# Thirteen tiles and TensorE for half of gV in the backward pass of a decode block

## The chip, the core and the metric

The kernel runs on one core of one Trainium2 chip. Its engines are TensorE (PE in the profile; its weight loads are PEld), VectorE (DVE), ScalarE (ACT), GpSimd (POOL) and SyncE (SP). Each follows its own list of instructions in order, and semaphores join the lists. Sixteen DMA engines move data between HBM and the on-chip SBUF. SP issues the loads, POOL issues the two large writes of each head, and ACT issues the writes of the weight gradients. The metric is the device time of the program in microseconds (us); lower is better.

## The reference

A transformer block for decoding, forward and backward, with two batch entries, one query position, D = 640, 32 heads of 128, a cache of 4096 positions and a ReLU layer of width 1728:

```python
def _fwd_reference(A_x, A_k_cache, A_v_cache, A_wq, A_wo, B_x, B_w1, B_w2):
    x = A_x
    h = x + attention(layernorm(x), A_k_cache, A_v_cache, A_wq, A_wo)
    h2 = h + relu(layernorm(h) @ B_w1) @ B_w2
    return h2
# attention: q = x@wq; s = q.k * 128**-0.5; p = softmax(s); o = p.v; out = o@wo
# outputs: h2, and the gradients of <h2, grad_out> with respect to
#          A_x, A_k_cache, A_v_cache, A_wq, A_wo, B_w1, B_w2
```

Everything is bfloat16. There are 64 pairs of batch entry and head. For each pair K and V are 1 MB each and are read, and gK and gV are 1 MB each and are written. With p a row of softmax weights, `gV[s] = p[s] * go` (go is the gradient of the head's output) and `gK[s] = gs[s] * q`, where `gs[s] = p[s] * (go.V[s] - dot)` needs V again.

## The kernel before

All tiles of 128 x 4096 bf16 (1 MB) live in a list of numbered homes that change their use: `ld` for loads, `g` for gK and gV on their way out, `f` for the weight gradients on theirs, `q` for late weights. `NBIG = 12` homes exist from the start, two more when the first pass ends (`big1`), one more (`big2`) and six more (`big3`) later. A queue written out by hand (`queue`, `pump`) issues the loads in order, each as soon as a home is free.

**First pass** (`p1_iter`, one iteration `i` per pair, over 64 pairs): `pair_transpose` turns K in four groups on TensorE (four fp32 transposes into one PSUM bank, copied out by ScalarE as `t_sb`; tag `XT` in SBUF). `pair_matvec` multiplies the transposed group with q (eight small matmuls). Softmax weights `ep` follow, VectorE forms `pk = K * p` in two halves (L464), and TensorE contracts `pk` with V (L457) and with a selector (L486).

**Background work** is written as generators (`bg`, `bg2`, `bg3`) that give out a piece after each step of the main work, paced by `RATES`, `RATE2`, `RATE3` and by `slot`, the number of row sums (L644 on VectorE) allowed at a step. For each batch entry `middle_gen` runs the layer between the passes, ending with `go_group` (one row sum a head), after which the second pass may take that head. `fin_gen` forms the weight gradients as outer products on TensorE (L928), copies them out on ScalarE (L934) and writes them; `gx_gen` and `mlp_out` do the last two row results.

**Second pass** (`p2_iter`, one turn `j` per pair). The order of the turns is `turns`: in each batch entry the last `KEPT` heads come first, because their V is still in SBUF from the first pass (6 in entry 0, 5 in entry 1). The other 53 turns load V again under the name `Wt`. Turns 0 to 11 run beside the first pass, one turn to two iterations; from turn 14 on the second pass is alone. A turn does, in six steps:

1. the last matvec of the turn before (group T3) and its `gsp` (L832); two broadcast matmuls (L841) copied out scaled as `rb` (L846); on POOL `pp`, a copy of the weights (L848); transposes T0; the first half of gK of the turn before (L819, VectorE);
2. the second half of gK of the turn before and its write (L860, POOL);
3. transposes T1, matvec of T0; 4. T2, matvec of T1; 5. T3, matvec of T2, first half of gV (VectorE);
6. second half of gV and its write (L881, POOL).

In turns 14 to 32 (`act = 8`) eight of the 32 columns of gV are formed by ScalarE instead, each by one scaled copy of `rb` (L880), the scale coming from `pa`, which POOL writes (L852):

```python
        outer_half(gV, c["rb"][:, 0:128], c["pp"], 1, act)
        for k in range(act):
            nc.scalar.activation(out=gV[:, NSC - act + k, :], in_=c["rb"][:, 0:128], func=ACT.Copy, scale=pa[:, k:k + 1])
        nc.gpsimd.dma_start(out=natural(out_3, b, h), in_=gV[:])
```

POOL's list at a turn's end and the next one's start is therefore: write of gV, `pp`, `pa`, write of gK.

Of the kernel before, what the change touches and what calls it, by code (L numbers as in the profile page):

```python
# [15 lines left out]
def kernel(  # L16
# [34 lines left out]
    GT = 8  # L51
# [4 lines left out]
    NMT = (32, 12)  # L56
# [6 lines left out]


# [15 lines left out]
    NBIG = 12  # L80
# [71 lines left out]
    neg_ident = const.tile([128, 128], BF16)  # L152
    nc.vector.tensor_scalar(out=neg_ident[:], in0=ident_bf[:], scalar1=-SCALE, scalar2=None, op0=ALU.mult)
# [3 lines left out]
    sel = const.tile([128, 2, 2, 64], BF16)  # L157
    nc.gpsimd.memset(sel[:], 0.0)
    for par in range(2):
        nc.gpsimd.affine_select(out=sel[:, par, :, :], in_=sel[:, par, :, :], compare_op=ALU.not_equal,  # L160
                                fill=1.0, base=-par, pattern=[[0, 2], [-2, 64]], channel_multiplier=1)
# [17 lines left out]
    xr = cols.tile([4 * ND, 128], BF16)  # L179
# [15 lines left out]

    gom = cols.tile([128, H, B, 2, 2], BF16)
# [3 lines left out]
    Uc = cols.tile([128, B, H], FP32)  # L200
# [3 lines left out]
    P_bf = cols.tile([128, B * H, NSC], BF16)  # L204
# [5 lines left out]
    nc.sync.dma_start(out=xr[0:2 * ND, :], in_=A_x.rearrange("b s (c p) -> (b s c) p", p=128))  # L210
    nc.sync.dma_start(out=xr[2 * ND:4 * ND, :], in_=grad_out.rearrange("b s (c p) -> (b s c) p", p=128))
# [11 lines left out]
    def ln_fwd(xs, nb, xh, rstd):  # L223

        def st(name, dt=FP32):
            return small.tile([128, nb], dt, tag=f"ln_{name}{nb}", bufs=1, name=f"ln_{name}")
# [7 lines left out]
        cent = small.tile([128, nb, ND], FP32, tag=f"ln_cent{nb}", bufs=1, name="ln_cent")  # L234
        nc.vector.tensor_tensor(out=cent[:], in0=xs, in1=bc(mean[:], ND), op=ALU.subtract)
        sq = small.tile([128, nb, ND], FP32, tag=f"ln_sq{nb}", bufs=1, name="ln_sq")
# [5 lines left out]
        y_bf = small.tile([128, nb, ND], BF16, tag=f"ln_y{nb}", bufs=1, name="ln_y")  # L242
# [33 lines left out]
    def ln_bwd(gh, xh, rstd, add, dst, nb):  # L276

        def t3(name):
            return small.tile([128, nb, ND], FP32, tag=f"lb_{name}{nb}", bufs=1, name=f"lb_{name}")
# [3 lines left out]
        mm = small.tile([128, 2, nb], FP32, tag=f"lb_mm{nb}", bufs=1, name="lb_mm")  # L283
# [5 lines left out]
        nm = small.tile([128, 2, nb], FP32, tag=f"lb_nm{nb}", bufs=1, name="lb_nm")  # L289
# [25 lines left out]
    nc.tensor.transpose(x_ps[:], xr[:], ident_bf[0:4 * ND, 0:4 * ND])  # L315
# [9 lines left out]
    nc.gpsimd.memset(hot[:, H - 1:H], 1.0)  # L325
    es = pkp.tile([128, B, H], FP32)
# [7 lines left out]
    def pair_rows(dst, src, hs, bs):  # L334

        n, nb = hs.stop - hs.start, bs.stop - bs.start
        t = pst([128, 2, n, nb], FP32, "mid", "pr_ps")
        for par in range(2):
            nc.tensor.matmul(t[:, par, :, :], lhsT=sel[:, par, :, :].rearrange("p c k -> p (c k)"),
                             rhs=src[:, hs, bs], start=True, stop=True)  # L340
        for c in range(2):
            rows = slice(64 * c, 64 * c + 64)
            for par in range(2):
                nc.vector.tensor_copy(out=dst[rows, hs, bs, par, c], in_=t[rows, par, :, :])
# [26 lines left out]
    def all_q():  # L371

        zero = small.tile([128, H * B], BF16, tag="zero", bufs=1, name="zero")
        nc.vector.memset(zero[:], 0.0)
# [7 lines left out]
        nc.tensor.matmul(q_ps[:].rearrange("p h b -> p (h b)"), lhsT=ident_bf[:], rhs=zero[:], start=True, stop=False)  # L382
# [12 lines left out]
    KEPT = (6, 5)  # L395
# [4 lines left out]
    u4 = cols.tile([128, 128], FP32)  # L400
# [14 lines left out]
    def pair_transpose(nat, g, dve=False, busy=0):  # L415
# [8 lines left out]
        t_sb = mats.tile([128, GT // 2, 128], FP32, tag="XT", bufs=5, name="t_sb")  # L424
# [24 lines left out]
    def p1_iter(i, dve_group, busy):  # L449
# [48 lines left out]
        if p is not None:  # L498

            bp, hp = pairs[i - 1]  # L500
            bhp = bp * H + hp
# [41 lines left out]
        if p is not None:  # L543
            pk_tile(1)
            if hp % OG == OG - 1:
                nc.vector.reciprocal(out=rt[:, bp, hp + 1 - OG:hp + 1], in_=totp)
            (nc.gpsimd if i < P2_AT else nc.vector).tensor_copy(out=P_bf[:, bhp, :], in_=ep[:, :, 0])
            pk_half(1)
            give(p["K"], "g" if i == P2_AT else None)
# [58 lines left out]
    def u_out(b):  # L608

        t = pst([128, H], FP32, "mid", "uc_ps")  # L610
        nc.tensor.matmul(t[:], lhsT=u4[:], rhs=fold[:], start=True, stop=True)
        nc.vector.tensor_tensor(out=Uc[:, b, :], in0=t[:], in1=rt[:, b, :], op=ALU.mult)


    def bcast_cols(colsrc, n, kc_of, dst):

        for c0 in range(0, n, 4):
            t = pst([128, 512], FP32, "bc", "bc_ps")
            w = 0
            for c in range(c0, min(n, c0 + 4)):  # L620
# [4 lines left out]
            nc.scalar.copy(out=dst[:, c0 * 128:c0 * 128 + w], in_=t[:, 0:w])  # L625
            yield
# [6 lines left out]
    def store_row(col_bf, n, dst):  # L633
# [3 lines left out]
        r = small.tile([16, 128], BF16, tag="orow", bufs=2, name="orow")  # L637
# [3 lines left out]
    def ttr(in0, in1, acc, width, kc=128, junk=None):  # L641
        if junk is None:
            junk = cols.tile([128, D], BF16, tag="junk", name="junk")
# [14 lines left out]
    def go_group(b, h0, h1, hbc):  # L658
# [3 lines left out]
        go32 = small.tile([128, GH], FP32, tag="go32", bufs=1, name="go32")  # L662
        for k in range(n):
            yield from turn()
            ttr(wo_t[:, h0 + k, :], hbc[:], go32[:, k:k + 1], D)
            yield 0.9
        nc.vector.tensor_copy(out=goc[:, hs, b], in_=go32[:, 0:n])
        pr = small.tile([128, GH], FP32, tag="pr", bufs=1, name="pr")
# [12 lines left out]
        ud = small.tile([128, GH], FP32, tag="ud", bufs=1, name="ud")  # L681
        nc.vector.tensor_tensor(out=ud[:, 0:n], in0=Uc[:, b, hs], in1=negdot[:, hs, b], op=ALU.mult)
        mg = small.tile([128, GH], FP32, tag="mg", bufs=1, name="mg")
# [7 lines left out]
    def mlp_out():  # L691

        ml32 = small.tile([128, ND, B], FP32, tag="ml32", bufs=1, name="ml32")
        nc.vector.memset(ml32[:], 0.0)
        for k in range(NW2):
            while free["q"] < 1:
                yield
# [12 lines left out]
        ml_bf = small.tile([128, ND, B], BF16, tag="ml_bf", bufs=1, name="ml_bf")  # L710
        nc.vector.tensor_copy(out=ml_bf[:], in_=ml32[:])
        y_bf = small.tile([128, B, ND], BF16, tag="y_bf", bufs=1, name="y_bf")
# [6 lines left out]
    def middle_gen(b):  # L719
        if o_next[0] < (b + 1) * H // OG:  # L720
            o_group()
        nc.vector.tensor_reduce(out=u4[:], in_=u_bank[0][:].rearrange("p (s d) -> p d s", s=4),
                                axis=AX.X, op=ALU.add)
        yield
# [7 lines left out]
        at_bf = small.tile([128, ND], BF16, tag="at_bf", bufs=1, name="at_bf")  # L732
        nc.vector.tensor_copy(out=at_bf[:], in_=asum[:, b, :])
        nc.vector.tensor_tensor(out=h1c[:, :, b], in0=xg32[:, b, :], in1=at_bf[:], op=ALU.add)
        h32 = small.tile([128, 1, ND], FP32, tag="h32", bufs=1, name="h32")
# [15 lines left out]
        if b == B - 1:  # L751
            ar_ps = pst([128, NFF, B], FP32, "mid", "ar_ps")
            for cf in range(NFF):
                for c in range(ND):
                    nc.tensor.matmul(ar_ps[:, cf, :], lhsT=w1_t[:, c, bass.ds(cf, 128, step=NFF)],
                                     rhs=x2c[:, c, :], start=(c == 0), stop=(c == ND - 1))
                yield 0.25
            nc.vector.tensor_scalar(out=arow[:, 0:NFF, :], in0=ar_ps[:], scalar1=0.0, scalar2=None, op0=ALU.max)
            if F_rem:
                nc.vector.tensor_copy(out=arow[:, NFF, :], in_=acol[:, NFF, :])  # L760
        mask = small.tile([128, NF], FP32, tag="mask", bufs=1, name="mask")
# [3 lines left out]
        fbc = cols.tile([128, Dff], BF16, tag="fbc", name="fbc")  # L765
        gx2 = small.tile([128, 1, ND], FP32, tag="gx2", bufs=1, name="gx2")
        gx2p = small.tile([128, ND, 3], FP32, tag="gx2p", bufs=1, name="gx2p")
        FW = Dff // 3
        spread_f = bcast_cols(one(ghfc, b), NF, f_kc, fbc)
        have = 0  # L770
        for k in range(3):
            while have < min(Dff, (k + 1) * FW):
                next(spread_f)
                have += 512
                yield
            for c in range(ND):
                yield from turn()
                ttr(w1_t[:, c, k * FW:(k + 1) * FW], fbc[:, k * FW:(k + 1) * FW], gx2p[:, c, k:k + 1], FW)
# [4 lines left out]
        hbc = cols.tile([128, D], BF16, tag="rowbc", name="hbc")  # L783
        yield from bcast_cols(one(gh1c, b), ND, lambda c: 128, hbc)
# [10 lines left out]
    def ga_gen():  # L795

        gbc = cols.tile([128, Dff], BF16, tag="fbc", name="gbc")
        for b in range(B):
            yield from bcast_cols(one(gc, b), ND, lambda c: 128, gbc[:, b * D:(b + 1) * D])
        for k in range(NW2):  # L800
# [3 lines left out]
            for c in range(k * FP, min(NF, (k + 1) * FP)):  # L804
                kc = f_kc(c)
                for b in range(B):
                    yield from turn()
                    ttr(t[0:kc, c - k * FP, :], gbc[0:kc, b * D:(b + 1) * D], ga[0:kc, b, c:c + 1], D, kc)
# [15 lines left out]
    def p2_iter(j, busy, act=0):  # L824

        c = S2[j] if j < NP1 else None
        p = S2[j - 1] if j >= 1 else None
        if p is not None:
            bp, hp = turns[j - 1]
            pair_matvec(p["dp"], p.pop("T3"), 3, gom[:, hp, bp, :, :])  # L830
            gsp = small.tile([128, NSC, 2], BF16, tag="gsp", name="gsp")
            nc.vector.scalar_tensor_tensor(  # L832
                out=gsp[:], in0=p["dp"][:, :, None].to_broadcast([128, NSC, 2]), scalar=negdot[:, hp, bp:bp + 1],
                in1=P_bf[:, bp * H + hp, :, None].to_broadcast([128, NSC, 2]), op0=ALU.add, op1=ALU.mult)
        if c is not None:
# [9 lines left out]
            rb = mats.tile([128, 256], BF16, tag="rb", bufs=4, name="rb")  # L845
            nc.scalar.activation(out=rb[:], in_=bank[:, 128:384], func=ACT.Copy, scale=rt[:, b, h:h + 1])  # L846
            pp = small.tile([128, NSC, 2], BF16, tag="pp", name="pp")
            nc.gpsimd.tensor_copy(out=pp[:], in_=P_bf[:, b * H + h, :, None].to_broadcast([128, NSC, 2]))  # L848
            c.update(rb=rb, pp=pp)
            if act:  # L850
                pa = small.tile([128, act], FP32, tag="pa", bufs=2, name="pa")
# [388 lines left out]
```

## Time and profile before

| what | value |
|---|---|
| time, median of 3 runs | 902.24 us (900.63 to 907.04) |
| profiled execution, its span from first to last instruction | 902.8 us |
| PE, DVE, ACT, POOL busy | 757.2, 687.2, 485.8, 198.7 us |
| moved by DMA | 362.89 MB, mean 402 GB/s |
| K, V, V again (`Wt`) loads | 64, 64, 53 of 1 MB |
| gK and gV writes | 64 and 64 of 1 MB |
| other writes (`ot`) | 14.91 MB |

The span of the profiled execution is its whole time; no other time is given for it. It lies within 0.1% of the median. A busy TensorE in this table is not TensorE at its peak: a transpose that waits for its bank or its tile counts in part. Rows of the profile's parts are quoted below as they stand; a line such as L423 is a line of the kernel before.

### The profile page before, as it was taken

How to read it: one execution, taken by the hardware profiler on the slowest of the kernel's cores; microseconds unless marked ns; L12 is line 12 of the kernel's file. 1: busy time of each engine (PE TensorE's matmuls, PEld its weight loads, DVE VectorE, ACT ScalarE, POOL GpSimd, SP SyncE). 2: the span in 40 equal slices, each digit the busy share in tenths (PEclk: the TensorE clock that was granted, in tenths of full speed). 3: DMA queues.
4: the chain of work that ended last, by engine and by line, in shares of the span. 5: the costliest groups of instructions: out<-in, count | busy, mean ns of one | idle time of the engine just before them, and what ended most of it. 6: DMA issues, size and time to landing. Idle time of an engine off the chain costs nothing.

```text
span 902.8 us, 24701 instructions
## 1 busy us (share of the span) xinstructions
PE 757.2 (84%) x10205; PEld 634.2 (70%) x10205; DVE 687.2 (76%) x1286; ACT 485.8 (54%) x1248; POOL 198.7 (22%) x349
## 2 busy tenths in 40 slices
PE   3999899899999898898968876878999778959880
PEld 3888788888888787787757765656767566645560
DVE  2566788777988796697778697769798448999982
ACT  0444344344565554464536677776577656637660
POOL 1344444343311011010012141122112111111120
PEclk9999999999999999798985555555557555555555
DMA  8999999999879999999999999999999999999995
GB/s 365 426 419 414 417 402 417 424 424 377 330 310 381 415 405 424 425 416 425 404 399 399 389 410 417 417 389 388 404 413 409 425 424 424 419 425 422 423 422 240
DMA packets 56256, 362.89 MB, mean 402 GB/s; under 512 B 5680, under 2 KB 11696, under 8 KB 15312
## 3 DMA queue, kind: packets, MB, share of 16 engines
q1 hardware_dynamic: 34704, 212.18, 57.8%
q0 software_dynamic: 18432, 134.23, 35.9%
q10 hardware_dynamic: 3008, 14.91, 4.1%
q8 instruction: 80, 1.31, 0.5%
q14 instruction: 32, 0.26, 0.1%
HBM read 212.16 MB, written 149.13 MB: 400 GB/s over the span
## 4 chain that ended last, share of the span: by engine, by line
PE 49%; DMA 21%; DVE 13%; ACT 11%; issue 5%; SPq 1%; POOL 0%; ACTq 0%; POOLq 0%; DVEq 0%
PE t_ps L423 21%; PE m_ps L457 10%; DMA Vt<-in_A_v_cache_dram 10%; ACT t_sb L428 3%; ACT gV L880 3%; DMA out_dram<-gK 3%; PE s_ps L436 3%; DVE gV L819 3%; PE u_ps L486 3%; PE dp_ps L436 3%; PE o_ps L928 3%; DMA wqs<-in_A_wq_dram 3%; DVE pk L464 2%; DVE gK L819 2%; DMA Kt<-in_A_k_cache_dram 2%
## 5 line engine op out<-in xcount | busy, mean ns | idle before, releaser
L428 ACT COPY t_sb<-t_ps 128x512 f32<-128x512 f32 x479 | 273.4, 585 | 211.0 <-PE t_ps L423 205.2
L436 PEld LDWEIGHTS <-t_sb 128*128 128x128 bf16 x4096 | 181.6, 103 | 62.0 <-ACT t_sb L428 27.4
L423 PE MATMUL t_ps<-ident_f,Wt 128*128 128x128 f32 x848 | 207.2, 396 | 0.4 <-ACT t_sb L428 0.4
L457 PE MATMUL m_ps<-pk,Vt 128*128 128x129 bf16 x2048 | 171.8, 223 | 16.1 <-DMA Vt<-in_A_v_cache_dram 14.7
L464 DVE TENSOR_TENSOR pk<-Kt,ep 128x2048 bf16<-128x2048 bf16 x128 | 156.5, 1223 | 33.5 <-PE m_ps L457 15.3
L423 PEld LDWEIGHTS t_ps<-ident_f,Wt 128*128 128x128 f32 x848 | 144.1, 206 | 33.2 <-issue 27.1
L819 DVE TENSOR_TENSOR gK<-rb,gsp 128x2048 bf16<-128x2048 bf16 x128 | 152.2, 1223 | 13.1 <-DMA out_dram<-gV 10.9
L423 PE MATMUL t_ps<-ident_f,Kt 128*128 128x128 f32 x1024 | 156.7, 287 | 4.4 <-DMA Kt<-in_A_k_cache_dram 4.3
L457 PEld LDWEIGHTS <-Vt 128*128 128x128 bf16 x2048 | 125.3, 99 | 46.5 <-issue 29.7
L819 DVE TENSOR_TENSOR gV<-rb,pp 128x2048 bf16<-128x2048 bf16 (+1 forms) x128 | 142.9, 1140 | 10.9 <-DMA out_dram<-gK 6.0
L423 PEld LDWEIGHTS t_ps<-ident_f,Kt 128*128 128x128 f32 x1024 | 113.7, 145 | 8.5 <-PE s_ps L436 2.6
L474 POOL COPY pk<-ep 128x16 bf16<-128x16 bf16 x80 | 83.2, 1042 | 161.0 <-ACT ep L512 90.5
L436 PE MATMUL dp_ps<-gom,t_sb 128*128 128x2 bf16 x2048 | 96.6, 168 | 17.8 <-ACT t_sb L428 17.1
L881 POOL DMA_DIRECT2D out_dram<-gV x64 | 34.2, 534 | 304.7 <-DVE gV L819 175.4
L436 PE MATMUL s_ps<-qm,t_sb 128*128 128x2 bf16 x2048 | 87.7, 164 | 1.2 <-DVE t_sb L426 1.2
L860 POOL DMA_DIRECT2D out_dram<-gK x64 | 34.0, 532 | 222.0 <-DVE gK L819 167.9
L571 ACT CAST MT<-m_ps 128x128 bf16<-128x128 f32 x64 | 17.1, 267 | 104.4 <-PE m_ps L457 104.3
L934 ACT CAST ot<-o_ps 128x512 bf16<-128x512 f32 (+4 forms) x160 | 70.2, 489 | 2.9 <-DMA out_dram<-ot 1.5
L832 DVE SCALAR_TENSOR_TENSOR gsp<-dp_ps,negdot,P_bf 128x64 bf16<-128x64 f32 x64 | 18.0, 282 | 50.8 <-PE dp_ps L436 50.0
L644 DVE CUSTOM_DVE_ANT_0 junk<-wo_t,hbc 128x640 bf16<-128x640 bf16 x64 | 52.7, 823 | 0.2
L846 ACT ACTIVATE rb<-dp_ps,rt 128x256 bf16<-128x256 f32 x64 | 30.1, 470 | 41.1 <-PE dp_ps L841 40.4
L644 DVE CUSTOM_DVE_ANT_0 gxj<-wqs,gqr 128x1024 bf16<-128x1024 bf16 x40 | 48.8, 1220 | 1.5 <-DMA wqs<-in_A_wq_dram 1.3
(200 smaller groups left out, 779.0 us busy)
## 6 DMA issues: line engine op xcount, KB each, us to landing
Kt<-in_A_k_cache_dram SPq DMA_DIRECT2D x64, 1024.0 KB, 15.3
Vt<-in_A_v_cache_dram SPq DMA_DIRECT2D x64, 1024.0 KB, 15.3
out_dram<-gV POOLq DMA_DIRECT2D x64, 1024.0 KB, 13.1
out_dram<-gK POOLq DMA_DIRECT2D x64, 1024.0 KB, 13.9
Wt<-in_A_v_cache_dram SPq DMA_DIRECT2D x53, 1024.0 KB, 12.4
wq_t<-in_A_wq_dram SPq DMA_DIRECT2D x5, 1024.0 KB, 9.0
wo_t<-in_A_wo_dram SPq DMA_DIRECT2D x4, 1280.0 KB, 18.1
wqs<-in_A_wq_dram SPq DMA_DIRECT2D x5, 1024.0 KB, 17.1
```

The lines of the kernel that those rows point to most:

```text
L423: nc.tensor.transpose(t_ps[:, j, :], natf[:, 2 * cc:2 * cc + 2, :].rearrange("p c k -> p (c k)"), ident_f[:])
L428: nc.scalar.copy(out=t_sb[:], in_=t_ps[:])
L436: nc.tensor.matmul(dst[:, sc:sc + 2], lhsT=v[:, j, :, par], rhs=vecs[:, par, :], start=(par == 0), stop=(par == 1))
L457: nc.tensor.matmul(r["m"][:, 0:129], lhsT=r["V"][:, sc, :], rhs=r["pk"][sc // HALF][:, sc % HALF, 0:129], start=(sc == 0), stop=(sc == NSC ...
L464: nc.vector.tensor_tensor(out=p["pk"][k][:, :, 0:128].rearrange("p s (a two) -> p s a two", two=2), in0=p["K"][:, sl, :].rearrange("p s (a ...
L474: nc.gpsimd.tensor_copy(out=col, in_=e)
L644: nc.vector.tensor_tensor_reduce(out=junk[0:kc, 0:width], in0=in0, in1=in1, scale=1.0, scalar=0.0, op0=ALU.mult, op1=ALU.add, accum_out=acc)
L819: nc.vector.tensor_tensor(out=pairs_view(dst[:, sl, :]), in0=row.rearrange("p (a two) -> p a two", two=2)[:, None, :, :].to_broadcast([128 ...
L846: nc.scalar.activation(out=rb[:], in_=bank[:, 128:384], func=ACT.Copy, scale=rt[:, b, h:h + 1])
L860: nc.gpsimd.dma_start(out=natural(out_2, bp, hp), in_=gK[:])
L881: nc.gpsimd.dma_start(out=natural(out_3, b, h), in_=gV[:])
L934: nc.scalar.copy(out=ot[0:P, k, n0:n0 + nn], in_=o_ps[0:P, 0:nn])
```

## The change

1. **Thirteen tiles.** `NBIG` goes from 12 to 13. Room is made by sharing small tiles (`sm`, `rows`, `scr`), by `P_bf` with 52 slots instead of 64, by fewer buffers (`XT` 5 to 4, `rb` 4 to 3, `pp`, `gsp` 3 to 2), and by fewer copies of small constants.
2. **Six V kept in each batch entry.** `KEPT` goes from (6, 5) to (6, 6): one `Wt` load fewer (52).
3. **TensorE and ScalarE form half of gV** in turns 14 to 32. POOL writes 16 weights into `wide`; four matmuls turn them to rows (`pt_ps`), ScalarE copies these out as `pt` (in an `XT` buffer); at the turn's end four groups of four matmuls with one row of weights each make 16 columns of gV in two PSUM banks, and four ScalarE copies of 128x512 bring them to gV.
4. **Four middle sums a head**: `slot` allows a row sum at four steps of a turn up to turn 32 instead of three. The built program has the last `go_group` sum of entry 1 in turn 34, before in turn 40, and what follows it moves forward by some six turns.
5. **Turns beside the first pass** (0 to 11) finish their own gK (`p2_whole`, `p2_tail`) in the iteration without a turn of its own.
6. Smaller: the layer's transposed activations (`arow`) come from 13 two-row matmuls in `fin_gen` instead of 65 matmuls with w1; the outer products for w2's gradient use 128 rows instead of 96, and one PSUM bank instead of three until the middle is over; the two small loads of x and grad_out are issued by ACT instead of SP.

```diff
-    NMT = (32, 12)
+    NMT = (32, 10)
-    NBIG = 12
+    NBIG = 13
-    KEPT = (6, 5)
+    KEPT = (6, 6)
-        t_sb = mats.tile([128, GT // 2, 128], FP32, tag="XT", bufs=5, name="t_sb")
+        t_sb = mats.tile([128, GT // 2, 128], FP32, tag="XT", bufs=4, name="t_sb")
...
+    def p2_gs(j):
+        p = S2[j]
+        bp, hp = turns[j]
+        pair_matvec(p["dp"], p.pop("T3"), 3, gom[:, hp, bp, :, :])
+        gsp = small.tile([128, NSC, 2], BF16, tag="gsp", bufs=2, name="gsp")
...
-    def p2_iter(j, busy, act=0):
+    def p2_iter(j, busy, pe=0):
...
-            if act:
-                pa = small.tile([128, act], FP32, tag="pa", bufs=2, name="pa")
-                nc.gpsimd.tensor_copy(out=pa[:], in_=P_bf[:, b * H + h, NSC - act:NSC])
+            if pe:
+                nc.gpsimd.tensor_copy(out=wide[:, :, 0:pe // 4, 0],
+                                      in_=P_bf[:, P_slot[(b, h)], NSC - pe:NSC].rearrange("p (q t) -> p t q", t=4))
             c["T0"] = pair_transpose(c["W"], 0, busy=busy)
+            if pe:
+                pt_ps = pst([128, 512], FP32, "gv", "pt_ps")
+                for t in range(4):
+                    nc.tensor.matmul(pt_ps[:, t * 128:(t + 1) * 128], lhsT=wide[:, t, :, :].rearrange("p q x -> p (q x)"),
+                                     rhs=ident_bf[:], start=True, stop=True)
+                pt = mats.tile([128, GT // 2, 128], FP32, tag="XT", bufs=4, name="pt")[:].bitcast(BF16)
+                pt = pt.rearrange("p j k -> p (j k)")
+                nc.scalar.copy(out=pt[:, 0:512], in_=pt_ps[:])
...
-        outer_half(gV, c["rb"][:, 0:128], c["pp"], 1, act)
-        for k in range(act):
-            nc.scalar.activation(out=gV[:, NSC - act + k, :], in_=c["rb"][:, 0:128], func=ACT.Copy, scale=pa[:, k:k + 1])
+        if pe < HALF:
+            outer_half(gV, c["rb"][:, 0:128], c["pp"], 1, pe)
+        for q in range(pe // 4):
+            gv_ps = pst([128, 4, 128], FP32, "gv", "gv_ps")
+            for t in range(4):
+                nc.tensor.matmul(gv_ps[:, t, :], lhsT=pt[32 * q:32 * q + 1, t * 128:(t + 1) * 128],
+                                 rhs=c["rb"][32 * q:32 * q + 1, 0:128], start=True, stop=True)
+            c0 = NSC - pe + 4 * q
+            nc.scalar.copy(out=gV[:, c0:c0 + 4, :], in_=gv_ps[:])
         nc.gpsimd.dma_start(out=natural(out_3, b, h), in_=gV[:])
...
+    def p2_tail(j):
+        p = S2[j]
+        bp, hp = turns[j]
+        gsp = p2_gs(j)
+        yield
+        gK = take("g", [128, NSC, 128], "gK")
+        outer_half(gK, p["rb"][:, 128:256], gsp, 0)
+        yield
+        outer_half(gK, p["rb"][:, 128:256], gsp, 1)
+        nc.gpsimd.dma_start(out=natural(out_2, bp, hp), in_=gK[:])
...
+    PE_GV = 16
     MIXED = {1: 2, 3: 1, 4: 1, 6: 1}
-    REST = {1: 1}
+    REST = {1: 2, 4: 1, 6: 1}
...
+            banks.update(sps=[2, 3], gv=[4, 5], o=[])
...
-            g2 = p2_iter(j, 0, 8 if i is None and j <= H else 0)
+            if i is not None and n + 1 < len(plan) and plan[n + 1][1] is None:
+                g2 = p2_whole(j)
+            else:
+                g2 = p2_iter(j, 0, PE_GV if i is None and j <= H and not late[0] else 0)
...
-                slot[0] = int(k in ((1, 3, 5) if j <= H else (1, 4)))
+                slot[0] = int(k in ((1, 2, 3, 5) if j <= H else (1, 4)))
```

## The prediction

> **What bounds the kernel now.** I read the page's forty slices first, then the busy times by stage, then single turns of the second pass in the timeline, since the change names that pass.
>
> ```profile
> PE   3999899899999898898968876878999778959880
> PEclk9999999999999999798985555555557555555555
> DMA  8999999999879999999999999999999999999995
> GB/s 365 426 419 414 417 402 417 424 424 377 330 310 381 415 405 424 425 416 425 404 399 399 389 410 417 417 389 388 404 413 409 425 424 424 419 425 422 423 422 240
> ```
>
> The reader sees a kernel that moves data nearly always: the best slices reach 424 to 426 GB/s, and 362.89 MB at 424 would take 856 us. The 47 us between that and the span of 902.8 us are all that smoother work can win. They sit in a few places: the start, 200 to 290 us, 440 to 700 us, and the end. TensorE's granted clock falls to half at about 476 us, where the second pass is alone, and stays there.
>
> ```profile
> core 0: us, PE busy (x) PEld busy (x) DVE busy (x) ACT busy (x) POOL busy (x), PEclk, DMA share, GB/s
> 200.00:290.00 90.00, 86.43 (x1509) 76.29 (x1506) 75.01 (x193) 49.46 (x137) 19.92 (x35) 1.00 0.90 349
> 440.00:476.00 36.00, 25.16 (x408) 22.05 (x407) 27.76 (x52) 14.59 (x39) 5.28 (x11) 0.86 0.99 396
> 476.00:532.00 56.00, 46.36 (x533) 41.38 (x531) 43.99 (x86) 39.53 (x107) 14.39 (x29) 0.50 1.00 396
> 532.00:627.00 95.00, 71.37 (x657) 58.72 (x658) 75.53 (x140) 69.47 (x188) 21.17 (x47) 0.54 1.01 403
> 627.00:700.00 73.00, 67.48 (x611) 52.50 (x611) 60.70 (x106) 50.52 (x116) 15.35 (x30) 0.57 1.00 409
> 700.00:890.00 190.00, 147.80 (x1294) 108.44 (x1292) 151.91 (x206) 108.43 (x229) 28.93 (x62) 0.54 1.01 423
> ```
>
> From 700 us on nothing can be won but bytes (423 GB/s). From 200 to 290 us TensorE is the bound and DMA stands still a tenth of the time, about 16 us. The writes of gV start turn 14 at 480.2 us and turn 32 at 622.3 us, so the 19 turns that the change rebuilds (14 to 32) take 476 to 627 us, 151 us or 7.9 us a turn. A turn moves 3 MB (V in, gK and gV out), 3.15e6 bytes or 7.4 us at 424 GB/s: DMA is the bound there, with little to spare. One such turn without much background shows what the engines need:
>
> ```profile
> 517.49 0.63 PE L622 MATMUL bc_ps<-ident_bf,ghfc 128*128 128x128 bf16 x4
> 517.92 1.06 PE L423 MATMUL t_ps<-ident_f,Wt 128*128 128x128 f32 x4
> ...
> 520.53 0.40 PE L436 MATMUL dp_ps<-gom,t_sb 128*128 128x2 bf16 x8
> 520.79 1.09 PE L423 MATMUL t_ps<-ident_f,Wt 128*128 128x128 f32 x4
> 521.68 0.40 PE L436 MATMUL dp_ps<-gom,t_sb 128*128 128x2 bf16 x8
> 522.62 0.37 PE L436 MATMUL dp_ps<-gom,t_sb 128*128 128x2 bf16 x8 [0.54 <-ACT t_sb L428]
> ...
> 523.02 1.91 PE L423 MATMUL t_ps<-ident_f,Wt 128*128 128x128 f32 x8
> ```
>
> ```profile
> 518.82 0.53 POOL L881 DMA_DIRECT2D out_dram<-gV  x1 [4.39 <-ACT gV L880]
> 519.34 0.48 POOL L848 COPY pp<-P_bf 128x64 bf16<-128x64 bf16 x1
> 519.76 0.72 POOL L852 CAST pa<-P_bf 128x8 f32<-128x8 bf16 x1
> ```
>
> ```profile
> 521.98 0.58 ACT L428 COPY t_sb<-t_ps 128x512 f32<-128x512 f32 x1 [0.56 <-PE t_ps L423]
> 522.46 2.45 ACT L880 ACTIVATE gV<-rb,pa 128x128 bf16<-128x128 bf16 x8
> ```
>
> From start to next start, at half clock: four transposes 0.89 us (520.79 to 521.68), eight matvecs 0.26 us, a matvec with the two broadcasts 0.40 us (522.62 to 523.02), four 128x128 bf16 matmuls with four different weights 0.43 us (517.49 to 517.92). TensorE's turn is 4 x 0.89 + 3 x 0.26 + 0.40 = 4.7 us, and turns here come every 6.4 us. TensorE has 1.7 us over, and the scaled copies at the turn's end hold up no TensorE instruction of their own turn.
>
> **Half of gV on TensorE.** Removed per turn: 2.45 us of ScalarE, 0.66 us of VectorE (the half gV of 1024 columns) and `pa`. Added: 20 small matmuls on TensorE, 5 copies on ScalarE (0.58 us each, 0.49 us behind each other), `wide` on POOL. VectorE's gain is spent: a fourth row sum at 0.82 + 0.08 us a turn costs as much. What is new is a loop through three engines, and the built order shows each link. POOL issues the write of gV after ScalarE's last copy, then `pp`, then `wide` of the next turn; TensorE needs `wide` for the four matmuls `pt_ps`, which stand right after T0, and all of T1, T2, T3 is queued behind them. Added up from the start of `pt_ps`:
> - `pt_ps` 0.43, then three times transposes and matvec, 3 x (0.89 + 0.26) = 3.45;
> - the four groups of gV. Each is 0.43 on TensorE; with two banks group 3 waits for the copy of group 1. Copies cannot start before a result is there (0.63 with a hand-over of 0.2) and end at 1.2, 1.7, 2.5 and 2.9 us. TensorE is free after 2.2, ScalarE after 2.9;
> - POOL: 0.53 for the write, 0.50 for `pp` (mean of 64), 0.39 for `wide` (mean of `pa`, whose form is nearest), and 0.2 for hand-overs: 1.6.
> Sum 0.43 + 3.45 + 2.9 + 1.6 = 8.4 us. TensorE's own work in it is 0.43 + 3.45 + 2.2 + 0.40 + 0.89 = 7.4 us, so it waits 1.0 us a turn. Both are above the 7.4 us of DMA or equal to it, at half clock.
>
> Background adds to that. In turns 14 to 21 it is small (70 one-column matmuls, 19 broadcasts: about 6 us of TensorE in eight turns), half of it in the wait: 8.7 us a turn, 70 us. In turns 22 to 32 the built order has 14 outer products of 512 columns and 14 of 128 (0.68 and 0.36 us at half clock around 608 us), 33 matmuls of row spreading and broadcasts, and the head groups: about 26 us in eleven turns or 2.4 a turn, of which 1.0 fills the wait: 9.8 us a turn, 108 us. Together 178 us against 151: +27. The low end is TensorE's work alone with copies fully hidden, 0.43 + 3.45 + 1.72 + 1.29 = 6.9, plus background 0.75 and 2.4: 61 + 102 = 163 us, +12. The high end has POOL at its slow rows and no background hidden, 8.8 + 0.75 and 8.8 + 2.4: 199 us, +48. I take +27, since the loop is worked out link by link from neighbours of the same shape.
>
> Here a rule speaks against the change. The row first: the four broadcasts above load four different weights and still follow each other at 0.108 us, so the loads are covered. The Trainium skill ("TensorE: Matmul & The Clock Gate", section "The mechanism") says a weight load overlaps running matmuls only when its row group differs, and the four of one gV group share theirs. By its figure for 128 columns (section "LDWEIGHTS", estimate 107 ns) a group would take 0.86 us instead of 0.43; the sum by it is in the last rival. The trace does not agree for full rows, and I go by the row.
>
> **What comes back.** DMA is not the bound in those turns, so at turn 32 more is done than before: all four free `ld` homes hold loaded V instead of about half, the queue of writes is empty (a write lands 13 us after its issue now, some 2 MB queued), a larger piece of out_7 is out, and one V load fewer is left. That is 1 + 2 + 1.5 + 0.5 MB, 5 MB or 11 to 12 us at 424 GB/s in the stage that DMA bounds to the end. Bounds 5 and 14; I take 11, which holds the saved load (2.5 us).
>
> **The rest.** The thirteenth tile lets DMA run one tile further before it stands still in 200 to 290 us: 1 MB or 2.5 us, between 0 and 2.5; I take 2.5. Finishing gK in the same pair moves 2.4 us of VectorE from the iteration with a turn to the one without, with its write one iteration earlier; by the 36 us from 440 at 396 GB/s (2.4 us lost) it is worth between -4 and +4 (VectorE's 27.76 of 36 us could also queue worse); I take -2. The first load leaves SP 0.8 us earlier: between 0 and -0.8, taken as -0.8. The 65 matmuls with w1 (4.5 us of TensorE) go, in the same turns as the loop, where the background estimate leaves them out. Fewer `XT`, `rb`, `pp`, `gsp` buffers cost nothing, since in the built order the reader of each old tile stands before the next writer by a turn; were that cover gone, ScalarE would wait one matvec, 0.26 us, a turn. More outer-product rows (128 for 96) cost nothing on TensorE, which streams columns.
>
> **The sum**: 902.8 + 27 - 11 - 2.5 - 2 - 0.8 = 913.5 us; the median runs stand 0.6 us below the profiled one, so I forecast 913 us.
>
> **Rivals.**
> - *Faster: the denser work brings the clock back.* At full clock the trace has four transposes in 0.45 us and a matvec group in 0.21 (around 567 us); the loop is then 0.22 + 3 x 0.66 + 2.7 + 1.6 = 6.5 us, below DMA's 7.4, and half of the 8.5 us that 476 to 627 us lose against 424 GB/s comes back: 902.8 - 4 - 2.5 - 5.3 = 891 us. For it: the clock is full through 300 us of the first pass. Against: from 627 to 700 us TensorE is busy 67.48 of 73.00 us and the clock is 0.57. The Trainium skill ("TensorE: Matmul & The Clock Gate", "What's actually happening") has the clock return after about 3.4 us of sustained activity; by that rule these 73 us should have been at full clock, and the trace shows they mostly were not.
> - *No change:* the low end of the loop with most of it repaid: 902.8 + 12 - 8 - 5.3 = 901.5 us. For it: DMA bounds the last 200 us whatever comes first. Against: 4 MB of free homes is all that can be filled in advance.
> - *Much slower:* weight loads of one row lie open. The 2x128 loads at L928 have a mean of 138 ns; 16 of them add 2.2 us to 1.72, 1.7 more than the 2.2 counted, 32 us in 19 turns: 913 + 32 - 3 = 942 us. It decides from about 30 ns a load, where the groups outlast the copies.
>
> **How the numbers follow.** Forecast 0.42, no change 0.32, faster 0.20, much slower 0.06. A measurement of this kernel tells about 1% from no change, 893 to 911 us: the faster rival lies below, no change within; of the forecast's own spread I leave all above 911. That is faster 0.20, same 0.32, slower 0.48. The range is 891 to 934: down to the faster case, up to the loop's high end (902.8 + 48 - 12 - 5.3 = 933.5).
>
> **What would show it.** Right: writes of gV in turns 14 to 32 come 8.5 to 10 us apart; DMA below 400 GB/s in that stage and at 424 after it; `pt_ps` matmuls waiting for POOL `wide`; clock near 0.5. The thirteenth tile: more than 349 GB/s in 200 to 290 us. Wrong: turns of 8 us or less there, a clock near 1.0, or TensorE held by the gV tile's last write.

## The result and the profile after

The changed kernel takes 945.96 us (median; 945.03 to 948.80) against 902.32 us (900.63 to 907.04) for the kernel before in the same comparison: a ratio of 1.0468 [1.0439, 1.0496]. It is slower by 4.7%; the forecast was 913 us with a range to 934. The profiled execution has a span of 943.7 us against 902.8 us. The page's slices of the kernel after, two of its rows:

```profile
PEclk9999999999999999989955555555558655565556
GB/s 380 418 404 411 409 400 409 419 417 379 345 263 423 421 422 422 422 422 422 404 375 303 308 326 294 303 277 348 345 355 424 423 423 424 426 423 419 420 420 289
```

Until about 476 us and from about 700 us on transfers run much as before (411 GB/s against 419 from 10 to 200 us, 422 against 423 from 700 to 890 us). Between them, in slices 21 to 30, where the kernel before had 388 to 417 GB/s, they fall to 277 to 375. The same stretches of the kernel after as windows (columns: us, busy time and instructions of PE, PEld, DVE, ACT and POOL, granted clock, DMA share, GB/s):

```profile
200.00:290.00 90.00, 85.98 (x1494) 75.98 (x1493) 72.03 (x185) 46.41 (x128) 19.46 (x35) 0.98 0.89 349
476.00:532.00 56.00, 44.44 (x488) 36.80 (x487) 31.68 (x65) 33.67 (x63) 12.39 (x23) 0.50 0.84 326
532.00:627.00 95.00, 71.27 (x707) 56.08 (x708) 54.92 (x113) 59.50 (x123) 20.10 (x37) 0.55 0.80 310
627.00:700.00 73.00, 58.23 (x541) 45.91 (x540) 49.89 (x95) 44.01 (x91) 14.95 (x27) 0.50 0.85 327
700.00:890.00 190.00, 155.54 (x1418) 113.86 (x1417) 158.24 (x219) 116.52 (x254) 32.10 (x66) 0.58 1.01 422
```

VectorE and ScalarE have less to do from 476 to 627 us than before, TensorE is no busier, and DMA stands still a sixth to a fifth of the time: no engine is full, which points to a chain through several engines. The issue of gV's writes by POOL gives the length of it. Turn 14 and turn 32, first in the kernel before (L881), then in the kernel after (L925):

```profile
480.22 0.53 POOL L881 DMA_DIRECT2D out_dram<-gV  x1 [5.40 <-ACT gV L880]
622.27 0.53 POOL L881 DMA_DIRECT2D out_dram<-gV  x1 [4.33 <-ACT gV L880]
481.50 0.53 POOL L925 DMA_DIRECT2D out_dram<-gV  x1 [5.36 <-ACT gV L924]
670.62 0.53 POOL L925 DMA_DIRECT2D out_dram<-gV  x1 [5.74 <-ACT gV L924]
```

| write of gV | before | after | difference |
|---|---|---|---|
| turn 14 | 480.2 us | 481.5 us | +1.3 |
| from turn 14 to turn 32 (18 steps) | 142.1 us, 7.9 a turn | 189.1 us, 10.5 a turn | +47.1 |
| from turn 32 to the end of the span | 280.5 us | 273.1 us | -7.4 |

All of the loss arises in the 19 turns that form half of gV on TensorE. The end of one of them, the next one and the start of a third, in rows chosen from the timeline of the kernel after:

```profile
489.83 2.40 DVE L841 TENSOR_TENSOR gK<-rb,gsp 128x2048 bf16<-128x2048 bf16 x2
490.08 0.53 POOL L925 DMA_DIRECT2D out_dram<-gV  x1 [4.51 <-ACT gV L924]
490.60 0.55 POOL L878 COPY pp<-P_bf 128x64 bf16<-128x64 bf16 x1
491.08 1.25 POOL L881 COPY wide<-P_bf 128x16 bf16<-128x16 bf16 x1
492.40 0.61 PE L887 MATMUL pt_ps<-ident_bf,wide 128*128 128x128 bf16 x4 [1.84 <-POOL wide L881]
496.27 0.62 PE L921 MATMUL gv_ps<-rb,pt 1*128 1x128 bf16 x8
497.55 1.07 PE L921 MATMUL gv_ps<-rb,pt 1*128 1x128 bf16 x8 [0.66 <-ACT gV L924]
499.54 0.53 POOL L925 DMA_DIRECT2D out_dram<-gV  x1 [6.48 <-ACT gV L924]
500.06 0.25 POOL L878 COPY pp<-P_bf 128x64 bf16<-128x64 bf16 x1
500.23 0.26 POOL L881 COPY wide<-P_bf 128x16 bf16<-128x16 bf16 x1
500.62 2.36 DVE L841 TENSOR_TENSOR gK<-rb,gsp 128x2048 bf16<-128x2048 bf16 x2
```

The chain is the forecast's: the last gV copy, POOL's write, `pp`, `wide`, `pt_ps`, three groups of transposes and matvecs, four groups of gV with one wait (0.66) for a bank. What is new is the same POOL instruction at 1.25 us in one turn and 0.26 us in the next. In the first VectorE runs the two halves of gK from 489.83 to 492.23; `pp` ends just after the first half, `wide` just after the second. In the other the halves of gK start at 500.62, when both copies are done. The tile `wide` as a whole (ns, min/median/max) and the waits from 476 to 676 us (us in total, times, longest):

```profile
L881 POOL COPY wide<-P_bf x19: 251/1245/1322, 470.2 to 660.3; 128x16 bf16<-128x16 bf16 x19
```

```profile
PEld L887 <- POOL wide L881: 24.0, 12, 2.9
PE pt_ps L887 <- POOL wide L881: 19.3, 11, 2.6
PE gv_ps L921 <- ACT gV L924: 13.8, 19, 1.2
```

Taken one by one, ten of the nineteen copies last 1.245 us or more, and each of these ends 0.105 to 0.114 us after the end of a half of gK on VectorE; the other nine last 0.251 to 0.262 us. The mean is 0.78 us. The Trainium skill ("SBUF — State Buffer", section "SBUF: two separate sides") says that VectorE with two SBUF inputs and a GpSimd instruction that reads SBUF share one pair of ports as an exclusive lock: whoever is second waits out the other's whole instruction. Its section "A bandwidth-pool intuition that's wrong (but worth ruling out)" measured a DMA issued by GpSimd as blocked until some 115 ns after the end of a VectorE copy. The trace agrees with the rule, and for a POOL copy it has nearly the same delay (105 to 114 ns); that of a DMA issue no run here shows.

### The profile page after: what moved, and what is told of

It is laid out like the page before. It is cut to its first block, busy times and chain, and to the rows that moved or that the text cites. A ratio compares the mean times of both kernels' runs of the same rounds, so it can differ in the third digit from the quotient of the medians.

```text
span 943.7 us, 25411 instructions
## 1 busy us (share of the span) xinstructions
PE 781.6 (83%) x10549; PEld 643.5 (68%) x10549; DVE 675.6 (72%) x1265; ACT 497.6 (53%) x1187; POOL 200.8 (21%) x350
## 4 chain that ended last, share of the span: by engine, by line
PE 49%; DVE 18%; DMA 15%; ACT 8%; issue 6%; POOL 2%; SPq 0%; ACTq 0%; POOLq 0%; DVEq 0%
PE t_ps L450 21%; DMA Vt<-in_A_v_cache_dram 9%; PE m_ps L484 8%; DVE rows L674 5%; DVE gV L841 4%; DVE gK L841 4%; DMA out_dram<-gK 3%; PE dp_ps L463 3%; DVE pk L491 3%; PE o_ps L992 3%; PE s_ps L463 3%; PE gv_ps L921 2%; PE u_ps L513 2%; ACT gV L924 2%; ACT t_sb L455 2%
## 5 line engine op out<-in xcount | busy, mean ns | idle before, releaser
L450 PE MATMUL t_ps<-ident_f,Wt 128*128 128x128 f32 x832 | 200.3, 389 | 0.6 <-ACT t_sb L455 0.6
L450 PEld LDWEIGHTS t_ps<-ident_f,Wt 128*128 128x128 f32 x832 | 137.0, 202 | 33.5 <-issue 24.0
L841 DVE TENSOR_TENSOR gV<-rb,pp 128x2048 bf16<-128x2048 bf16 x109 | 130.7, 1218 | 6.1 <-DMA out_dram<-gK 5.3
L925 POOL DMA_DIRECT2D out_dram<-gV x64 | 34.1, 534 | 343.9 <-DVE gsp L852 115.4
L999 ACT CAST ot<-o_ps 128x512 bf16<-128x512 f32 (+3 forms) x152 | 69.6, 491 | 11.9 <-PE o_ps L992 8.8
L898 POOL DMA_DIRECT2D out_dram<-gK x53 | 28.2, 531 | 158.2 <-DVE gK L841 129.3
L674 DVE CUSTOM_DVE_ANT_0 rows<-wo_t,rows 128x640 bf16<-128x640 bf16 x64 | 52.4, 819 | 0.4
L674 DVE CUSTOM_DVE_ANT_0 rows<-w_t,rows 128x640 bf16<-128x640 bf16 (+2 forms) x58 | 45.4, 784 | 6.2 <-ACT rows L654 5.8
## 6 DMA issues: line engine op xcount, KB each, us to landing
out_dram<-gK POOLq DMA_DIRECT2D x64, 1024.0 KB, 10.5
```

Source lines behind the costliest of these rows:

```text
L450: nc.tensor.transpose(t_ps[:, j, :], natf[:, 2 * cc:2 * cc + 2, :].rearrange("p c k -> p (c k)"), ident_f[:])
L674: nc.vector.tensor_tensor_reduce(out=junk[0:kc, 0:width], in0=in0, in1=in1, scale=1.0, scalar=0.0, op0=ALU.mult, op1=ALU.add, accum_out=acc)
L841: nc.vector.tensor_tensor(out=pairs_view(dst[:, sl, :]), in0=row.rearrange("p (a two) -> p a two", two=2)[:, None, :, :].to_broadcast([128 ...
L999: nc.scalar.copy(out=ot[0:kp, k, n0:n0 + nn], in_=o_ps[0:kp, 0:nn])
```

## The experiments

Theory L: one loop through TensorE, ScalarE and POOL sets the turn; each link counts with its own duration, and the copy into `wide` counts with what VectorE makes of it. Rival theories put the loss into the number of gV groups alone, into the clock, or into the other parts of the change. All ratios are to the kernel before on the same chip, whose median was 902.3 to 904.6 us in all groups.

**1. All of gV back on VectorE.**

```
-    PE_GV = 16
+    PE_GV = 0
```

> The changed kernel with PE_GV = 0: turns 14 to 32 form all of gV on VectorE, everything else as changed (banks, buffers, thirteen tiles, four sums). Theory L (the loop TensorE, ScalarE, POOL through wide sets the pace of turns 14 to 32): these turns fall from 10.5 us to about 8 us, DMA goes back above 400 GB/s from 476 us on, time 898 to 905 us. Rival M (the four sums a turn, the single bank for outer products and the smaller buffer counts cost a good part of the 44 us): time 915 us or more.

Measured: 898.69 us (897.22 to 900.63), ratio 0.9927 [0.9901, 0.9952]. Turns 14 to 32 come 7.8 us apart, at 404 to 417 GB/s. With all of gV on VectorE the rest of the change is a gain of 0.7%; against that, TensorE's half of gV costs 47 us.

**2. ScalarE's eight scaled copies put back into the changed kernel**, with `pa`, the three banks for outer products, and no `wide`:

```
-        for q in range(pe // 4):
-            ...
+        for k in range(act):
+            nc.scalar.activation(out=gV[:, NSC - act + k, :], in_=c["rb"][:, 0:128], func=ACT.Copy, scale=pa[:, k:k + 1])
```

> The changed kernel with ScalarE's eight scaled copies of before in place of the TensorE half, and the three banks for outer products of before; thirteen tiles, six kept V, four sums, own gK beside the first pass stay. Theory L: 893 to 900 us, a little below before by the saved load and the extra tile. Rival M: near 915 us as with no TensorE part at all. If the thirteenth tile and the saved load bring nothing, 900 to 905 us.

Measured: 901.80 us (898.45 to 905.29), ratio 0.9970 [0.9946, 0.9994]; 8.1 us a turn. With the old division of gV the rest of the change is worth about 0.3%, less than the 893 to 900 us expected. What takes the rest of the gain in this version was not shown.

**3. The kernel before with TensorE's half of gV alone** (one bank for outer products until the middle work is over, `rb` in three buffers, as the change has them):

```
-        for k in range(act):
-            nc.scalar.activation(...)
+        for q in range(pe // 4):
+            gv_ps = pst([128, 4, 128], FP32, "gv", "gv_ps")
+            ...
```

> The kernel before with only the TensorE half of gV put in (with its two banks, one bank for outer products until the middle is over, and three rb buffers); twelve tiles, (6, 5) kept, three sums a turn. Theory L: the cost comes along, 935 to 950 us, turns 14 to 32 at 10 us or more. Rival M: within 10 us of before, 900 to 912 us.

Measured: 963.01 us (961.55 to 965.08), ratio 1.0634 [1.0587, 1.0680]; 10.5 us a turn, 321 to 322 GB/s from 476 to 700 us. The part carries its loss with it into the other kernel, and more: the time is 13 us above the expected range. Turns 14 to 32 are 46.5 us longer than before; the rest of the 59 us lies ahead of turn 14 (487.0 us) and behind turn 32 (287.7 us to the end), and was not explained.

**4. `wide` of the next turn filled a turn ahead**, before POOL issues this turn's gV write:

```
+            if pe and j < H:
+                fill_wide(j + 1, pe)
```

> The changed kernel, but POOL writes wide of the next turn before the write of gV of this turn, so that the link from ScalarE's last copy through POOL to pt_ps is gone. Theory L: TensorE's wait for wide (24 us in 12 turns) goes, 946 - 24 + a few us of lead not gained = 922 to 930 us; pt_ps no longer waits for POOL. Rival N (TensorE's own work and its hand-overs with ScalarE are the bound, the wait for wide only shows where the slack lies): 938 us or more.

Measured: 922.39 us (920.09 to 926.11), ratio 1.0194 [1.0150, 1.0239]; 9.0 us a turn, and `pt_ps` waits for `wide` no more. VectorE still stretches the copy (259/426/1008 ns), but nobody waits for it. The wait for a bank is unchanged (13.8 us, 19 times). About half of the loss was the wait for `wide`, with all that POOL does ahead of it.

**5. The copy into `wide` on ScalarE, at its old place.**

```
-                nc.gpsimd.tensor_copy(out=wide[:, :, 0:pe // 4, 0],
-                                      in_=...
+                nc.scalar.copy(out=wide[:, :, 0:pe // 4, 0],
+                                      in_=...
```

> The changed kernel with the copy into wide on ScalarE in place of POOL, at the same place in the program. Theory L with VectorE's hold (the POOL copy takes 1.25 us because a two-input multiplication of VectorE runs beside it): ScalarE's copy takes 0.2 to 0.35 us whatever VectorE does, the turn in 14 to 32 falls from 10.5 to 8.8 to 9.4 us, and the time is 915 to 928 us, as when wide was written ahead (922). Rival (the strided write into wide is slow on any engine, or the wait goes to another link of the loop): the copy still takes about 1.2 us, or pt_ps waits for something else as long, and the time is 938 to 948 us.

Measured: 923.22 us (920.19 to 926.01), ratio 1.0225 [1.0152, 1.0298]; 9.1 us a turn. Its row of the tile `wide`:

```profile
L881 ACT COPY wide<-P_bf x19: 249/252/261, 466.3 to 636.7; 128x16 bf16<-128x16 bf16 x19
```

ScalarE needs 0.25 us every time, eighteen of the nineteen times beside a half of gK or gV on VectorE. So neither the strided write nor the tile is slow; it is POOL beside VectorE. The 23 us won are more than the hold, though: as in run 4, POOL's write of gV and `pp` no longer stand ahead of `wide`. The hold of `wide` by itself, 0.78 - 0.25 us in 18 steps, is some 10 us of it by the trace; no run takes away the hold alone.

**6. Eight columns on TensorE instead of sixteen**, `wide` on POOL at its place (`PE_GV = 8`).

> The changed kernel with 8 columns of gV on TensorE in place of 16: two groups of four matmuls and two copies a turn, which the two banks hold, VectorE does the other eight; POOL still fills wide at its place. Theory L (one loop through TensorE; each gV group and each wait for a bank lengthens the turn by its own duration): two groups (0.43 us each) and the wait for ScalarE's copies (13.8 us in 19 turns, 0.7 each) leave the loop, so a turn falls from 10.5 to about 8.9 to 9.2 us and the time to 916 to 925; the wait for wide stays (20 to 26 us in 19 turns). Rival (pt_ps alone, behind its wide, holds the turn and the gV groups lie beside other work): 938 to 948.

Measured: 924.60 us (920.20 to 926.54), ratio 1.0229 [1.0191, 1.0268]; 9.3 us a turn. Its row of `wide`:

```profile
L881 POOL COPY wide<-P_bf x19: 208/1210/1267, 469.7 to 639.8; 128x8 bf16<-128x8 bf16 x19
```

Half the elements take as long where VectorE is busy: the length is VectorE's, not the copy's. `pt_ps` still waits for it 27.3 us (20 to 26 were expected, and turns of 8.9 to 9.2 us), and the two gV groups that are gone take 1.2 us a turn with them.

**7. Eight columns and `wide` ahead.**

> 8 columns on TensorE, and wide filled a turn ahead by POOL. Theory L: from the 9.04 us a turn of the version with wide ahead and 16 columns, 1.5 us more go; the loop is then near 7.6 us, under the 7.8 to 7.9 us that transfers allow, so transfers set the turn again: 7.8 to 8.2 us a turn, over 395 GB/s in 476 to 700 us, 896 to 906 us. Rival (what is left above before comes from pt_ps and the extra weight loads at half clock, not from the number of gV groups): 915 to 924.

Measured: 901.53 us (897.20 to 903.52), ratio 0.9947 [0.9913, 0.9982]; 7.9 us a turn. Windows of this run, columns as above:

```profile
476.00:532.00 56.00, 49.95 (x612) 44.44 (x610) 48.74 (x102) 36.64 (x70) 21.08 (x32) 0.59 1.00 409
532.00:627.00 95.00, 74.53 (x801) 59.52 (x799) 79.31 (x155) 63.35 (x139) 27.05 (x44) 0.61 0.98 399
627.00:700.00 73.00, 57.56 (x645) 45.43 (x643) 52.87 (x80) 47.53 (x95) 13.28 (x27) 0.71 1.01 414
```

Transfers are the bound again. The two causes add up, as links of one loop do, down to the turn that transfers allow:

| | `wide` on POOL, in its place | `wide` out of the loop |
|---|---|---|
| 16 columns on TensorE | 945.96 us, 10.5 a turn | 922.39 us, 9.0 a turn |
| 8 columns on TensorE | 924.60 us, 9.3 a turn | 901.53 us, 7.9 a turn |

**8. What the small parts do.** The kernel before once more, profiled on the chip of the runs 5, 9 and 10:

> The kernel before, unchanged, profiled on the chip that runs the others of this group. Theory S (the small parts of the change are real, and were hidden because the one profile of before had faster transfers in its first 200 us, 419 GB/s against 411): here too 10 to 200 us runs at 409 to 413 GB/s, 200 to 290 us at 330 to 338, the first gV write is issued at 273 to 276 us and turn 14's at 484 to 488. Theory N (the small parts are worth nothing): first gV write at 267 to 269 us and turn 14's at 479 to 482, as in the profile of before.

One run: 909.49 us, span 907.7 us. Transfers ran at 419 GB/s from 10 to 200 us here too, and at 331 from 200 to 290 us; the first gV write came at 270.7 us and turn 14's at 485.6. This fits neither theory whole: the first stretch speaks against S, the first write lies between the two, the rest speaks for S. The same program differs by 5 us at turn 14 from one profile to the next.

**9. The kernel before without ScalarE's eight copies** (`8 if ...` becomes `0`):

> The kernel before, with ScalarE's eight scaled copies in turns 14 to 32 given back to VectorE. If VectorE sets the turn there, each turn grows by the eighth of a 1.2 us multiplication each half saves (half of one half, about 0.6 us, in 19 turns): 910 to 918 us. If transfers set the turn (396 to 403 GB/s there), no change: 899 to 905. If ScalarE's copies themselves were in the way, 893 to 898.

Measured: 911.04 us (907.11 to 915.20), ratio 1.0071 [1.0038, 1.0104]. The number is the first theory's, the place is not: turns 14 to 32 come 7.8 us apart, no slower than before, and the loss arises after turn 32 (286.4 us to the end against 280.5). The likely reading is that VectorE's time is taken from the background, which then comes late; this was not shown by itself.

**10. The version of run 1 with twelve tiles and six and five kept V.**

> The changed kernel without TensorE's half of gV (VectorE forms all of it), and with twelve tiles and six and five V kept, as before. If the thirteenth tile and the one more kept V make the gain of the version with all of gV on VectorE (898.7 us in the earlier group), this one is at 902 to 906 us, and its rate in 200 to 290 us falls from 348 to 333 to 338 GB/s. If the gain is from gK in its own pair, the four sums and the absent copies, it stays at 897 to 900.

Measured: 905.33 us (899.50 to 907.58), ratio 1.0011 [0.9978, 1.0043], 341 GB/s from 200 to 290 us. Against run 1 (0.9927) the thirteenth tile and the kept V are worth 0.8%, 7 to 8 us (by the two intervals 4 to 11), the whole of that version's gain. The profiled executions of the two differ by 4.4 us: 1.0 until turn 14, 3.3 after turn 32.

**11. The version of run 1 with three row sums a head in place of four.**

```
-                slot[0] = int(k in ((1, 2, 3, 5) if j <= H else (1, 4)))
+                slot[0] = int(k in ((1, 3, 5) if j <= H else (1, 4)))
```

> All of gV on VectorE (898.7 us in the first group), and three middle sums a head in place of four. If the fourth sum lets finished work come back earlier (the background), three cost 2 to 6 us: 901 to 905. If VectorE is the tighter engine there (86 of 95 us busy in 532 to 627), fewer sums relieve it: 893 to 897.

Measured: 915.09 us (913.44 to 916.17), ratio 1.0129 [1.0102, 1.0156]: 2% or 18 us worse than run 1, three times the larger guess. Row sums over `wo_t` from 476 to 627 us in run 1:

```profile
L674 DVE CUSTOM_DVE_ANT_0 rows<-wo_t,rows 128x640 bf16<-128x640 bf16 x30 | 24.6, 820 | 0.4
```

and in this run, from 476 to 627 and from 627 to 700 us:

```profile
L674 DVE CUSTOM_DVE_ANT_0 rows<-wo_t,rows 128x640 bf16<-128x640 bf16 x21 | 17.2, 819 | 0.2
L674 DVE CUSTOM_DVE_ANT_0 rows<-wo_t,rows 128x640 bf16<-128x640 bf16 x11 | 9.0, 817 | 0.0
```

Its turns 14 to 32 are the quickest of all (7.7 us), but the sums end some turns later, and transfers then fall to 362 GB/s from 627 to 700 us and 399 from 700 to 890 (417 and 418 in run 1). Late sums alone do not explain it: in the kernel before the last of them starts at 686.3 us (688.8 here, 643.8 in run 1), and there transfers keep 409 GB/s from 627 to 700 us. Here VectorE also forms all of gV, and the outer products have one bank until the sums are done; which of the two makes three sums too few was not tested.

**12. The version of run 1 with three banks for outer products** in turns 14 to 32 and no `wide` tile at all (`banks.update(sps=[2, 3], gv=[], o=[4, 5])`):

> All of gV on VectorE, and the banks that TensorE's half would have used are given to the outer products of the background in turns 14 to 32, three in place of one, with no wide tile filled. If the one bank held the background back, it comes earlier and the time falls by 2 to 5 us below 898.7: 893 to 897. If not, 897 to 901.

Measured: 898.37 us (896.60 to 902.25), ratio 0.9940 [0.9918, 0.9961]: with four sums a head the one bank did not hold the background back. Runs 1, 7 and 12 beat both kernels most, the one before by 0.5 to 0.7%, and can't be told apart. So TensorE's part, at eight columns (run 7), costs nothing once its loop is short, but it also wins nothing over VectorE forming all of gV.

## Why the prediction was wrong

The sign and the mechanism were right: of what it named as signs, `pt_ps` waits for POOL's `wide`, transfers fall below 400 GB/s in that stage and stand at 422 after it, and the clock is 0.50 to 0.55. Only the writes of gV, 8.5 to 10 us apart in the forecast, came 10.5 apart. The profiled execution missed the sum by 943.7 - 913.5 = 30 us. Between the two writes the forecast had 18/19 of 27, 25.6 us, and 47.1 came: 21.5 of the 30 us are in **the term of the loop**. That step failed in two places.

*The POOL term.* "0.39 for `wide` (mean of `pa`, whose form is nearest)" was 0.78. The mean hid two kinds of copy, as that row of the kernel before could have told, and as the one `pa` in the forecast's timeline (0.72) did:

```profile
L852 POOL CAST pa<-P_bf x19: 179/195/809, 468.4 to 616.7; 128x8 f32<-128x8 bf16 x19
```

Minimum and maximum stand four to one: seven of the nineteen take 0.72 to 0.81 us, each over a row sum of VectorE. In the changed kernel ten of nineteen are held, and by the longer multiplication for gK. The forecast had slow POOL rows in its high end only. The error is 0.39 x 18 = 7 us.

*The background that "fills the wait".* The forecast let 14 us of background vanish in the wait of 1.0 us a turn (half of 6 us, and 1.0 in each of eleven turns). But TensorE works in order and waits at `pt_ps`; only what stands between the last gV group and `pt_ps` can run in the wait. In the trace 19 of the 28 outer-product matmuls and 31 of the 46 for row spreading and broadcasts of these turns run behind `pt_ps`, where they lengthen the loop. The wait stayed open: 19.3 us. That is 14 x 18/19 = 13 us, and 7 + 13 is nearly all of the 21.5.

The trace of the changed kernel bears this out, measured from the start of one turn's `pt_ps` to the next one's (18 steps, mean 10.65 us). The first matmul of gV comes after 5.19 us; the forecast's links give 3.88, and turns without background show 3.88 to 3.93. The last copy of gV ends 2.97 us later (2.9 in the forecast), the write's issue 0.82 after that, and `pp` and `wide` 1.21 after that (0.89). Then 0.45 us pass until `pt_ps`, 0.06 where it had waited. So background and its own waits lengthen a turn by 1.31 us behind `pt_ps` and 0.39 ahead of it.

With both mended, after the fact, the prediction's links give the turns of every version (background 32 us in 19 turns, 1.7 a turn): 8.4 + 0.39 + 1.7 = 10.5 us for the changed kernel (10.5 measured); TensorE's own work 7.4 + 1.7 = 9.1 with `wide` out of the loop (9.0 and 9.1); with two gV groups, whose copies end at 1.7 instead of 2.9 us, 8.4 + 0.39 - 1.2 + 1.7 = 9.3 (9.3); and with both, 7.4 - 1.3 + 1.7 = 7.8, under the 7.9 at which transfers set the turn (7.9). The links themselves, `pt_ps`, groups, transposes, gV's copies, were of the right size, as the steps above show.

**What comes back**: -11 was forecast, -7.4 came. Run 1 has no slack to use in turns 14 to 32 and still needs only 275.7 us after turn 32, run 10 with twelve tiles 279.0. So 279.0 - 275.7 = 3.3 us belong to the kept V and the tile, 280.5 - 279.0 = 1.5 to other parts of the change, and at most 275.7 - 273.1 = 2.6 to work done ahead in the slack, where 8.5 was forecast. Even these 2.6 are not shown to come from it, since run 2, with little slack (8.1 us a turn), also needs 273.0. What keeps the rest from coming back was not shown.

**The thirteenth tile, gK in its own pair, the earlier load**: -5.3 until turn 14 was forecast, +1.3 came, and "more than 349 GB/s in 200 to 290" was not met (349). One profile can't carry that: over the profiles of all runs turn 14's write stands at 480.2 to 487.0 us in the four with the first pass of before (mean 483.8), and at 479.8 to 482.9 in the nine with the changed pass and thirteen tiles (mean 481.5). That is about -2.4 us, inside the spread, and run 10 with the changed pass and twelve tiles stands at 481.5 too, so it is not shown to be the tile. By whole times the tile and the kept V earn 7 to 8 us (runs 1 and 10); for these two the forecast had 2.5 and 2.5.

**"VectorE's gain is spent: a fourth row sum"** was counted as a cost only. Where VectorE forms all of gV it is worth 18 us (run 11); no run takes it out of the changed kernel itself.

**The rivals.** The clock did not return: 0.50 to 0.58 in the changed kernel. The rival of no change needed the loop's low end and most of it repaid; the loop came out at its high end. The 942 us of the last rival are near the result by luck, since its mechanism did not occur: eight one-row matmuls in a row show 0.62 us, no more than the forecast counted. The range took the loop's high end with 12 us of repayment; the loop came out there, and the repayment did not.

## What to carry to other kernels

A wait in an engine's list can only be filled by work that stands before the waiting instruction; count the background by its place in the list before it is set off against a wait. Read minimum and maximum beside the mean of a short POOL instruction, and look for what VectorE does beside the slow ones: a quarter of a microsecond became one and a quarter, and in a loop through several engines that counts wherever nothing fills the wait, so such a copy belongs on ScalarE or a turn ahead. The loss of 47 us fell to nothing against the kernel before once the loop was shorter than the transfers of a turn (run 7, with half the columns); shorten a new loop to below the old bound before judging the idea, and then compare it with leaving the idea out, which here was as fast (run 1).

## What the hardware showed that was not expected

Two-input multiplications of VectorE held a POOL copy of 16 elements a partition for up to their whole length (0.25 to 1.32 us), while ScalarE did the same copy in 0.249 to 0.261 us beside them; the held copies ended 0.105 to 0.114 us after VectorE. Row sums of VectorE held them too (seven copies of 0.88 to 0.89 us in run 4). And a program without any edit moved its turn 14 by 5 us, and the rate of 200 to 290 us from 349 to 331 GB/s, between two profiles, so that effects of that size are read from several runs.
